# Turning the first two token tiles behind the last expert's second half: float32r transposes in place of float32 identity matmuls

## The chip, the cores and the metric

One core of a Trainium2 chip runs the whole program in one launch. The metric is device time in microseconds of that core; the median of several executions is compared. Engines by their short names: PE is TensorE (PEld its weight loads), DVE VectorE, ACT ScalarE, POOL GpSimd, SP SyncE.

## The reference

Three stages follow one another on 1536 tokens (2 batches of 768) of 512 numbers.

1. A decayed linear attention, 8 heads of 64, gives the rows `x`.
2. A mixture of 8 experts with one expert for each token. `e` is the largest gate logit, or the expert of the token before where the local gate is open:

```python
p = softmax(x[b, s] @ w_gate)
h = np.maximum(x[b, s] @ w1[e], 0.0)        # 512 -> 1024
out[b, s] = p[e] * (h @ w2[e])              # 1024 -> 512
```

3. A mixing stage, for all tokens: `gate = sigmoid(causal 5-tap convolution of x with conv_w)`, `val = x @ w_val`, result `(gate * val) @ w_out`.

The change lies at the seam of stages 2 and 3: the first 256 tokens of stage 3 need their expert's answers, turned so that the 512 features lie on partitions.

## The kernel before

**Experts.** Tokens are sorted by expert into slots (up to 240 slots an expert are computed here, in two tiles of 128). For each expert `e` in 0 to 7, `up(e, j)` makes the hidden rows in four pieces, and `down(e, 0)` and `down(e, 1)` (line 768) make the answers of its first and second tile of slots: 24 matmuls each of 128x128 against 128x512, which add up in one PSUM tile `py`. Numbers are split in a high and a low float32r part, so each product is three float32r matmuls. `down_out` (line 778) scales `py` on ACT into `yo` and writes it to `ys` in HBM by a DMA that ACT issues (line 782).

**The mixing stage** takes the tokens in their own order again, 256 (two tiles) at a time, n = 0 to 5. `fetch(n)` gathers two tiles of answers from `ys` by indirect DMAs that POOL issues (line 907); `turn(n)` transposes them on PE into PSUM (line 917, float32r, through `nc.tensor.transpose`); `parts(n)` splits them (ACT line 928, DVE line 930); `whole(n)` and `taps(n)` feed the convolution, which `conv(n, ...)` adds up on DVE (line 951); `value(n)` is 48 matmuls (line 965), `gate(n)` multiplies, `project(n, t)` is the last product (line 991).

**The first two tiles take a shortcut.** They don't wait until the last expert's answers are in HBM:

- `early_answers` (line 789), during the last expert's `up`, gathers the answers of these 256 tokens that earlier experts gave into `yg` (line 792). Tokens of the last expert get a row of zeros. It also makes two one-hot matrices `oh0` and `oh1` on DVE, which say what token has which slot of the last expert.
- `early_answers_turn` (line 800) turns `yg` into two PSUM tiles `pt0` (line 804): for each of 4 blocks of features and 2 tiles an ordinary float32 matmul of the 128x128 block with the identity `ident`, 8 calls. The first call in a PSUM bank has `start=True`, and none has `stop`.
- `last_parts` (line 807) splits the last expert's first tile of answers into two float32r parts on ACT and DVE, and `last_place(0, ...)` (line 812) adds them to `pt0` through `oh0`: 8 float32r matmuls (line 815). `last_place(1, [yo])` adds the second tile, from `yo`, as 4 float32 matmuls through `oh1`.

`pt0` then stands in for `turn(0)`. The mixing stage begins with `fetch(1)`, then `parts(0)`, `whole(0)`, `taps(0)` and `value(0)`, and `turn(1)` is put into `value(0)` after 40 of its 48 matmuls.

**Order.** In both parts the instructions of PE, ACT, DVE and SP stand in the order in which the code calls them (`manual_schedule`); in the mixing stage POOL does too. Semaphore waits are derived from the tiles that instructions read and write. `fetch(1)` reads all of `ys`, so it waits for the last write of `ys`; this wait stands in semaphore instructions on POOL's queue ahead of the gather. The first gather's own instruction waits for PE's last matmul of line 815.

**The last expert's end**, before (lines 855 to 879), in the order of the calls: `down(7, 0)`, `down_out(7, 0)`, `last_parts`, `early_answers_turn`, `down(7, 1)`, `last_place(0)`, `down_out(7, 1)`, `last_place(1)`.

Of the kernel before, what the change touches and what calls it, by code (L numbers as in the profile page):

```python
# [9 lines left out]
F32R = mybir.dt.float32r  # L10
# [11 lines left out]
P = 128  # L22
# [19 lines left out]
def fused_kernel(ctx, tc, qkv, lam, wgl, w1, w2, wv, cw, wo, out, dbg=None):  # L42
    nc = tc.nc
# [44 lines left out]
    ident = const.tile([P, P], F32, name="ident")  # L88
# [3 lines left out]
    identr = const.tile([P, P], F32R, name="identr")  # L92
# [101 lines left out]
    def from64_b(dst, a, m):  # L194
        nc.vector.scalar_tensor_tensor(dst, m.bitcast(F32), MIN64, a.bitcast(F32), op0=ALU.is_ge, op1=MUL)
# [3 lines left out]
    def split64_a(n):  # L199
        src, c0 = (wv if n < 4 else wo), (n % 4) * 512  # L200
        raw = wraw_p.tile([P, 1024], U32, name="wraw64", tag="wraw")
        nc.sync.dma_start(raw, src[:, c0:c0 + 512].bitcast(U32))
        w64_t[n] = from64_a(raw)

    def split64_b(n):
        dst, c0 = (wv_t if n < 4 else wo_t), (n % 4) * 512
        w = f64_p.tile([P, 512], F32, name="f64w", tag="f64w")
        from64_b(w, *w64_t.pop(n))
        sl = slice(c0, c0 + 512)
        nc.scalar.copy(dst[:, 0, sl], w)  # L210
        nc.gpsimd.tensor_tensor(dst[:, 1, sl], w, dst[:, 0, sl].bitcast(F32), op=SUB)
# [12 lines left out]
    def first_hi(n, cs=slice(0, 1024)):  # L224
        w = (w1_t if n < 4 else w2_t)[0]
        if len(w) == n % 4:
            w.append(split_hi(raw_t[n], None, cs))
        else:
            split_hi(raw_t[n], w[n % 4], cs)

    def first_lo(n, cs=slice(0, 1024)):
        split_lo(raw_t[n], (w1_t if n < 4 else w2_t)[0][n % 4], cs)
# [392 lines left out]
    def all_indices():  # L625
        for g in range(ET, NT):
            indices(g)
        nc.vector.tensor_tensor(idx, idxa, pidx[:, 2 * E:4 * E], op=ADD)
# [85 lines left out]
    def x_fetch(e):  # L714
        xr = xr_p.tile([P, 2, XW], F32, name="xr", tag="xr")
        for t in range(2):
            nc.gpsimd.indirect_dma_start(  # L717
                xr[:, t, :], None, xd, bass.IndirectOffsetOnAxis(ap=idx[:, 2 * e + t:2 * e + t + 1], axis=0))
        xr_t[e] = xr

    def softmax_fetch(e):
        xs = xh_p.tile([P, 2, E], F32, name="xsm", tag="xsm", bufs=1)

        rows = keep.tile([P, 2], I32, name="rows")
        nc.vector.tensor_scalar(rows, idx[:, 2 * e:2 * e + 2], float(XW // E), float(DM // E), op0=MUL, op1=ADD)
        for t in range(2):
            nc.gpsimd.indirect_dma_start(
                xs[:, t, :], None, xd.rearrange("r (a n) -> (r a) n", n=E), bass.IndirectOffsetOnAxis(ap=rows[:, t:t + 1], axis=0))
        return xs
# [13 lines left out]
    def softmax_of(e, xs):  # L743

        pe = xh_p.tile([P, 2], F32, name="pe", tag="pe")
        nc.gpsimd.tensor_copy(pe, xs[:, :, e])
        pe_t[e] = pe

    def w1_chunk(e, k):
        w1_t.setdefault(e, []).append(split(raw_load(w1[e * P:(e + 1) * P, k * FF:(k + 1) * FF])))  # L750

    def w2_chunk(e, j):
        raw = raw_t[4 + j] if e == 0 else raw_load(w2[e * P:(e + 1) * P, j * 1024:(j + 1) * 1024])
        w2_t.setdefault(e, []).append(split(raw))

    def up(e, j, hhs):
        ph = ps_h.tile([P, 2, CAP], F32, name="ph", tag="ph")[:, :, 0:C1]
        xh = xh_t[e]
        for fi, a, b, k, first, last in halves(e == j == 0):
            f = 2 * j + fi  # L760
            nc.tensor.matmul(ph[:, fi, :], w1_t[e][k][:, a, f * P:(f + 1) * P],  # L761
                             xh[:, b, k].rearrange("p t n -> p (t n)")[:, 0:C1], start=first, stop=last)
        hh = hidden[(e * (KF // 2) + j) % len(hidden)]
        nc.scalar.activation(hh[:, 0, :, 0:C1], ph, AF.Relu)  # L764
        nc.vector.scalar_tensor_tensor(hh[:, 1, :, 0:C1], ph, 0.0, hh[:, 0, :, 0:C1].bitcast(F32), op0=ALU.max, op1=SUB)  # L765
        hhs.append(hh)
# [20 lines left out]
    early, pt0 = {}, []  # L787

    def early_answers():
        early["yg"] = yg = whl_p.tile([P, 4, DM], F32, name="yg0", tag="whl")  # L790
        for t in range(2):
            nc.gpsimd.indirect_dma_start(yg[:, t, :], None, ys[0:ZROW + 1, :],
                                         bass.IndirectOffsetOnAxis(ap=yslot0[:, t:t + 1], axis=0))
        early["y"] = whl_p.tile([P, 4, DM], F32R, name="yhl", tag="whl")
        for t in range(2):
            oh = early["y"][:, 2 + t, 0:CAP]
            nc.vector.tensor_scalar(oh, iota256, last[:, t:t + 1], None, op0=ALU.is_equal)
            early[f"oh{t}"] = oh if t == 0 else oh.bitcast(F32)

    def early_answers_turn():  # L800
        pt0.extend(ps_x.tile([P, 2, CAP], F32, name=f"pt{i}", tag="px") for i in range(2))
        for k in range(KD):
            for t in range(2):
                nc.tensor.matmul(pt0[k // 2][:, k % 2, t * P:(t + 1) * P], early["yg"][:, t, k * P:(k + 1) * P], ident,
                                 start=(k % 2 == t == 0), stop=False)

    def last_parts(py):
        y, pe = early["y"], pe_t[E - 1][:, 0:1]
# [3 lines left out]
    def last_place(t, srcs):  # L812
        for k in range(KD):
            for src in srcs:
                nc.tensor.matmul(pt0[k // 2][:, k % 2, :], src[:, k * P:(k + 1) * P], early[f"oh{t}"],  # L815
                                 start=False, stop=(t == k % 2 == 1))

    ordered = {mybir.EngineType.Activation, mybir.EngineType.DVE, mybir.EngineType.PE, mybir.EngineType.SP}
    with tc.manual_schedule(engines=ordered):
        parts_of_answers = answers()  # L820
        for e in range(E):
            hhs = []
            if 0 < e < E - 1:
                x_fetch(e + 1)
            for j in range(KF // 2):
                up(e, j, hhs)
                if e == 0 and j == 0:
                    all_indices()
                    softmax_of(0, softmax_fetch(0))
                    x_fetch(1)  # L830
                    first_hi(5)
                    first_lo(5)
                elif e == 0 and j == 1:
                    nc.sync.dma_start(ys[ZROW:ZROW + 1, :].rearrange("o (a n) -> (o a) n", a=2), zero[0:2, :])
                elif e == 1 and j == 0:

                    nc.scalar.activation(sig, warm_sb[:, 0:1], AF.Sigmoid)
                elif e == E - 1 and j == 1:
                    early_answers()
                if e > 0:  # L840
                    w2_chunk(e, j)
                elif 0 < j < 3:
                    w2_chunk(e, j + 1)
                if 2 <= e < 5 and j == 1:
                    next(parts_of_answers)
                if e == 0 and j == 3:
                    split64_a(0)
                if j == 3 and e > 0:
                    split64_b(e)
                    if e == 3:  # L850
                        nc.sync.dma_start(cw_raw, cw.bitcast(U32))
                        from64_b(cw_sb.rearrange("p k j -> p (k j)"), *from64_a(cw_raw))
            if e + 1 < E:
                w1_chunk(e + 1, 0)
            py = down(e, 0, hhs)
            if e + 1 < E:
                w1_chunk(e + 1, 1)
                x_turn(e + 1)
            down_out(e, 0, py)
            if 1 <= e < 1 + NOV:  # L860
                for t in range(2):
                    r0 = (E + e - 2) * CAP + t * P
                    for c0 in range(0, DM, 256):
                        nc.sync.dma_start(ys[r0:r0 + P, c0:c0 + 256], zero)
            if e == E - 1:
                last_parts(py)
                early_answers_turn()
            py = down(e, 1, hhs)
            if e + 1 < E:
                w1_chunk(e + 1, 2)  # L870
                w1_chunk(e + 1, 3)
                if e == 0:
                    split64_b(0)
                split64_a(e + 1)
            if e == E - 1:
                last_place(0, [early["y"][:, a, :] for a in range(2)])
            yo = down_out(e, 1, py)
            if e == E - 1:
                last_place(1, [yo])
# [317 lines left out]
```

## Time and profile before

| | us |
|---|---|
| median of 3 runs | 346.55 (346.36 to 347.4) |
| profiled execution, its own time | 346.0 |
| its span in the profile | 344.1 |
| PE busy | 334.5 (97%) |
| DVE busy | 272.1 (79%) |
| ACT busy | 197.2 (57%) |
| POOL busy | 65.0 (19%) |

The span is what the profiler saw of engines; 1.9 us of the execution's own time lie around it. The engines work at once, so the busy times don't add up. Ends of matmuls are modelled, and neighbours overlap in the rows, so the distance from start to start is the safer reading of how long a matmul holds PE. A matmul on float32 data shows as two matmuls and two weight loads, one on float32r data as one.

### The profile page before, as it was taken

What the parts mean: (1) busy time and instruction counts of PE and PEld (TensorE: products, weight loads), DVE (VectorE), ACT (ScalarE), POOL (GpSimd) and SP (SyncE); (2) the same over time, 40 slices, a digit from 0 to 9 for tenths busy, and PEclk for the clock granted to TensorE, in tenths of its full rate; (3) what the DMA queues carried; (4) which work ended last, traced back from release to release, by engine and by line L of the source; (5) the groups of instructions that cost most, each with busy time, mean ns of one, the idle gap of its engine ahead of it and who ended that gap; (6) DMA issues with size and microseconds to landing.
All of it is one profiled execution on the core that took longest, in us unless ns stands there. A gap on an engine that the chain in (4) does not pass through costs nothing.

```text
span 344.1 us, 7024 instructions
## 1 busy us (share of the span) xinstructions
PE 334.5 (97%) x2686; PEld 296.4 (86%) x2686; DVE 272.1 (79%) x600; ACT 197.2 (57%) x418; POOL 65.0 (19%) x84
## 2 busy tenths in 40 slices
PE   6999999999999999999999999999999899999995
PEld 3888888879989889899898898998988889899884
DVE  5788999988798688788987877778740799977980
ACT  1577677864557645745756457457441567664731
POOL 3000000020463121321411214201320650000000
PEclk9999999999999999999999999999999999999999
DMA  6997983473778888799698887987521542011012
GB/s 245 403 350 294 302 311 96 126 225 114 225 234 289 275 282 280 235 318 286 196 354 275 270 296 223 356 259 239 198 63 61 139 132 71 35 56 63 30 63 98
DMA packets 24819, 72.00 MB, mean 209 GB/s; under 512 B 3398, under 2 KB 6732, under 8 KB 23628
## 3 DMA queue, kind: packets, MB, share of 16 engines
q1 hardware_dynamic: 20020, 59.87, 51.5%
q0 software_dynamic: 2304, 7.42, 7.4%
q10 hardware_dynamic: 2456, 4.20, 3.2%
q8 instruction: 23, 0.38, 0.5%
q14 instruction: 16, 0.13, 0.1%
HBM read 57.79 MB, written 13.68 MB: 208 GB/s over the span
## 4 chain that ended last, share of the span: by engine, by line
PE 91%; DMA 3%; DVE 2%; ACT 1%; SPq 0%; issue 0%; POOL 0%; ACTq 0%
PE py L773 26%; PE ph L761 25%; PE po L991 10%; PE pv L965 9%; PE ps L273 4%; PE po L297 3%; PE po L290 3%; PE rt L337 2%; PE rt L335 2%; DMA qk<-in_qkv_dram 2%; PE st L317 1%; PE px L737 1%; DMA yg<-ys,yslot 1%; PE pt L917 1%; PE pt L815 1%; PE px L450 1%
## 5 line engine op out<-in xcount | busy, mean ns | idle before, releaser
L168 DVE TENSOR_TENSOR whl<-wraw,whl 128x1024 fp32r<-128x1024 f32 (+1 forms) x68 | 81.8, 1219 | 17.5 <-ACT whl L164 17.5
L773 PE MATMUL py<-whl,hh 128*128 128x512 f32 x384 | 92.7, 396 | 0.0
L761 PEld LDWEIGHTS ph<-xh,whl 128*128 128x128 f32 x768 | 87.8, 190 | 1.1 <-ACT xh L473 0.4
L761 PE MATMUL ph<-xh,whl 128*128 128x240 f32 x768 | 88.4, 276 | 0.2 <-ACT xh L473 0.2
L773 PEld LDWEIGHTS py<-whl,hh 128*128 128x128 f32 x384 | 70.9, 188 | 16.0
L164 ACT CAST whl<-wraw 128x1024 fp32r<-128x1024 f32 (+1 forms) x68 | 66.3, 994 | 4.7 <-ACT yo L780 2.9
L764 ACT ACTIVATE hh<-ph 128x480 fp32r<-128x480 f32 x32 | 18.3, 573 | 41.3 <-PE ph L761 40.6
L951 DVE SCALAR_TENSOR_TENSOR gt<-yt,cw_sb,gt 128x256 f32<-128x256 f32 x96 | 39.0, 476 | 1.1 <-ACT gt L943 1.1
L965 PE MATMUL pv<-yh,wv_t 128*128 128x256 f32 x288 | 35.6, 283 | 0.0
L965 PEld LDWEIGHTS pv<-yh,wv_t 128*128 128x128 f32 x288 | 35.1, 191 | 0.5 <-ACT yh L928 0.2
L991 PE MATMUL po<-wo_t,gh 128*128 128x512 f32 (+1 forms) x156 | 34.6, 378 | 0.0
L991 PEld LDWEIGHTS po<-wo_t,gh 128*128 128x128 f32 x156 | 27.3, 188 | 5.8 <-DVE gh L981 0.8
L765 DVE SCALAR_TENSOR_TENSOR hh<-ph,hh 128x480 fp32r<-128x480 f32 x32 | 21.0, 656 | 12.8 <-ACT hh L764 12.8
L780 ACT ACTIVATE yo<-py,pe 128x512 f32<-128x512 f32 x16 | 11.1, 695 | 18.7 <-PE py L773 18.7
L717 POOL DMA_INDIRECT xr<-xd,idx x14 | 16.6, 1186 | 12.5 <-PE px L737 6.9
L273 PE MATMUL ps<-qk 64*128 64x128 f32 x176 | 15.3, 295 | 0.0
L443 POOL DMA_INDIRECT xr<-xd,idx x2 | 2.7, 1338 | 64.5 <-DMA wraw<-in_w_dram 64.2
L191 POOL TENSOR_TENSOR f64a<-f64a,f64s 128x512 f32<-128x512 f32 (+1 forms) x9 | 12.4, 1380 | 10.8 <-DMA wraw<-in_w_dram 9.1
L907 POOL DMA_INDIRECT yg<-ys,yslot x10 | 11.2, 1121 | 17.1 <-DVE yh L930 11.2
L280 DVE TENSOR_TENSOR sm<-ps,dm 128x512 f32<-128x512 f32 x22 | 14.1, 681 | 0.2 <-PE ps L273 0.2
L928 ACT CAST yh<-pt 128x512 fp32r<-128x512 f32 x12 | 6.6, 588 | 11.7 <-PE pt L917 10.3
L297 PE MATMUL po<-sm,qk 128*64 128x128 f32 x192 | 13.1, 279 | 0.0
(175 smaller groups left out, 426.1 us busy)
## 6 DMA issues: line engine op xcount, KB each, us to landing
wraw<-in_w_dram SPq DMA_DIRECT2D x64, 512.0 KB, 5.8
qk<-in_qkv_dram SPq DMA_DIRECT2D x9, 1024.0 KB, 5.9
ys<-yo ACTq DMA_DIRECT2D x16, 256.0 KB, 6.2
xd<-xtok SPq DMA_DIRECT2D x12, 260.0 KB, 2.5
ys<-warm_sb SPq DMA_DIRECT2D x24, 128.0 KB, 5.1
out_dram<-oo SPq DMA_DIRECT2D x11, 256.0 KB, 2.0
qk<-in_qkv_dram SPq DMA_DIRECT2D x5, 512.0 KB, 6.2
wraw<-in_w_val_dram SPq DMA_DIRECT2D x4, 512.0 KB, 4.7
```

The source lines that it names most:

```text
L164: nc.scalar.copy(hl[:, 0, cs], raw[:, cs])
L168: nc.vector.tensor_tensor(hl[:, 1, cs], raw[:, cs], hl[:, 0, cs].bitcast(F32), op=SUB)
L273: nc.tensor.matmul(ps_t[g][hl][:, hp, :], t[r, half, 256 + c0:256 + c0 + P], t[r, half, c0:c0 + P], start=True, stop=True)
L297: nc.tensor.matmul(po_t[g][hl * D:(hl + 1) * D, hp, :], qk_t[g][:, 3, h * D:(h + 1) * D], sm_t[g][:, hl, hp, :], start=(c == 0), stop=(c = ...
L717: nc.gpsimd.indirect_dma_start(xr[:, t, :], None, xd, bass.IndirectOffsetOnAxis(ap=idx[:, 2 * e + t:2 * e + t + 1], axis=0))
L761: nc.tensor.matmul(ph[:, fi, :], w1_t[e][k][:, a, f * P:(f + 1) * P], xh[:, b, k].rearrange("p t n -> p (t n)")[:, 0:C1], start=first, sto ...
L764: nc.scalar.activation(hh[:, 0, :, 0:C1], ph, AF.Relu)
L765: nc.vector.scalar_tensor_tensor(hh[:, 1, :, 0:C1], ph, 0.0, hh[:, 0, :, 0:C1].bitcast(F32), op0=ALU.max, op1=SUB)
L773: nc.tensor.matmul(py, hhs[f // 2][:, a, f % 2, t * P:(t + 1) * P], w2_t[e][f // 2][:, b, (f % 2) * DM:(f % 2 + 1) * DM], start=(n == 0), ...
L951: nc.vector.scalar_tensor_tensor(gt[:, k, :], yt[:, b, k, c0 + j:c0 + j + 256], cw_sb[:, k, j:j + 1], gt[:, k, :], op0=MUL, op1=ADD)
L965: nc.tensor.matmul(pv[:, mi, :], wv_t[:, a, k * DM + m * P:k * DM + (m + 1) * P], yh[:, b, k, :], start=first, stop=last)
L991: nc.tensor.matmul(po, gh[:, a, k, t * P:(t + 1) * P], wo_t[:, b, k * DM + cs.start:k * DM + cs.stop], start=(i == 0), stop=(i == 11))
```

## The change

`early_answers_turn` is called later, between `down(7, 1)` and `last_place(0)`, and its 8 calls are float32r transposes (`is_transpose=True` against `identr`, views of the same bytes as float32r) with the same `start` and `stop` flags. The `last_place` matmuls add to what the transposes left in PSUM, as they did to what the matmuls left. No other call is moved.

```diff
         for k in range(KD):
             for t in range(2):
-                nc.tensor.matmul(pt0[k // 2][:, k % 2, t * P:(t + 1) * P], early["yg"][:, t, k * P:(k + 1) * P], ident,
-                                 start=(k % 2 == t == 0), stop=False)
+                nc.tensor.matmul(pt0[k // 2][:, k % 2, t * P:(t + 1) * P].bitcast(F32R),
+                                 early["yg"][:, t, k * P:(k + 1) * P].bitcast(F32R), identr,
+                                 start=(k % 2 == t == 0), stop=False, is_transpose=True)
...
             if e == E - 1:
                 last_parts(py)
-                early_answers_turn()
             py = down(e, 1, hhs)
...
             if e == E - 1:
+                early_answers_turn()
                 last_place(0, [early["y"][:, a, :] for a in range(2)])
             yo = down_out(e, 1, py)
```

## Rows read from the trace of the kernel before

**Rows 1.** The page: busy times, and the chain that ended last by engine.
```profile
PE 334.5 (97%) x2686; PEld 296.4 (86%) x2686; DVE 272.1 (79%) x600; ACT 197.2 (57%) x418; POOL 65.0 (19%) x84
...
PE 91%; DMA 3%; DVE 2%; ACT 1%; SPq 0%; issue 0%; POOL 0%; ACTq 0%
```

**Rows 2.** The chain of waits in order of time: start, length, engine, tile, line, count.
```profile
142.92 0.64 PE px L737 x8
143.56 5.67 PE py L773 x24
...
165.66 0.63 PE px L737 x8
...
256.54 1.78 PE pt L804 x16
258.32 5.61 PE py L773 x24
263.93 2.79 PE pt L815 x16
...
268.79 4.37 DMA yg<-ys,yslot
...
273.81 6.77 PE pv L965 x56
```

**Rows 3.** Line 815, from `yo`: count, duration ns min/median/max, first and last start.
```profile
L815 PE MATMUL pt<-yhl,yo x8: 379/379/475, 264.7 to 266.3; 128*128 128x256 f32 x8
```

**Rows 4.** Line 737, the float32r transposes of the experts' rows.
```profile
L737 PE MATMUL px<-identr,xr x56: 221/248/255, 96.8 to 234.2; 128*128 128x128 f32 x56
```

**Rows 5.** Timeline around the seam: start, length, instructions [idle before <-releaser].
```profile
263.77 1.11 PE L815 MATMUL pt<-yhl 128*128 128x256 f32 x8
263.97 0.69 ACT L780 ACTIVATE yo<-py,pe 128x512 f32<-128x512 f32 x1 [5.56 <-PE py L773]
264.69 0.33 ACTq L782 DMA_DIRECT2D ys<-yo  x1
...
264.72 1.99 PE L815 MATMUL pt<-yhl,yo 128*128 128x256 f32 x8
...
266.51 5.02 PE L965 MATMUL pv<-yh,wv_t 128*128 128x256 f32 x40
...
266.78 1.27 DVE L930 TENSOR_TENSOR yh<-pt,yh 128x512 fp32r<-128x512 f32 x2
...
267.53 0.96 POOL L907 DMA_INDIRECT yg<-ys,yslot  x1 [11.15 <-DVE yh L930]
...
271.37 0.46 PE L917 MATMUL pt<-identr,yg 128*128 128x128 f32 x4
...
272.49 0.69 DVE L930 TENSOR_TENSOR yh<-pt,yh 128x512 fp32r<-128x512 f32 x1
...
273.30 0.51 PE L917 MATMUL pt<-identr,yg 128*128 128x128 f32 x4 [1.47 <-DMA yg<-ys,yslot]
...
274.46 0.69 DVE L930 TENSOR_TENSOR yh<-pt,yh 128x512 fp32r<-128x512 f32 x1 [1.28 <-ACT yh L928]
```

**Rows 6.** Line 782 (255 to 268 us), the last expert's writes: issue to landing.
```profile
DMA to landing us min/median/max: 2.0/2.0/2.0
```

**Rows 7.** Line 907 (266 to 272 us): POOL's queue, and landings.
```profile
L907 POOLq EVENT_SEMAPHORE  x3: 17/43/43, 266.7 to 270.9; - x3
...
DMA to landing us min/median/max: 3.3/3.8/4.4
```

**Rows 8.** POOL's timeline: two other gathers released by PE.
```profile
144.33 1.50 POOL L717 DMA_INDIRECT xr<-xd,idx  x1 [1.58 <-PE px L737]
...
166.56 1.54 POOL L717 DMA_INDIRECT xr<-xd,idx  x1 [0.67 <-PE px L737]
```

**Rows 9.** Line 717 (142 to 146 us): the queue instruction ahead of the first of these.
```profile
L717 POOLq EVENT_SEMAPHORE  x1: 17/17/17, 143.6 to 143.6; - x1
```

**Rows 10.** Stretches: length, busy (count) of PE, PEld, DVE, ACT, POOL; PEclk, DMA, GB/s.
```profile
233.60:234.40 0.80, 0.80 (x10) 0.74 (x9) 0.80 (x1) 0.80 (x2) 0.06 (x1) 1.00 0.53 164
```

## The prediction

> **What bounds the kernel now.** I read the busy table first, then the chain of waits, then the timeline of the few microseconds around the edit. PE is busy 97% of the span and is 91% of the chain that ended last [rows 1]; a microsecond of PE work that is taken out anywhere on that chain is a candidate for a microsecond of time. The chain around the edit [rows 2] shows where that is true. From 256.54 to 266.7 it is PE without a gap: the 16 passes of line 804 (1.78 us), the second half of the answers (5.61), the placing of line 815 (2.79). Then it leaves PE: it goes through a gather of the next two tiles from HBM (4.37 us from issue to landing), and comes back to PE at the second half of that tile pair's transposes. The timeline [rows 5] shows the same as a wait: PE does its 40 matmuls of line 965, transposes the first gathered tile at 271.37, and then stands idle 1.47 us until the second tile has landed (273.30). From there on the chain is PE again.
>
> So there are two things to follow through the edit: how much earlier PE reaches that wait, and how much earlier the wait ends. The later of the two sets the end.
>
> The timeline names DVE line 930 as the releaser of the first gather (267.53). I don't believe it: the gather is called before that line and depends on nothing that it writes. What it does depend on is the last write of `ys`, issued at 264.69 [rows 5], landed 2.0 us later [rows 6], at 266.69; and POOL's first semaphore instruction for it runs at 266.7 [rows 7]. The other condition is PE's last placing, which ends at 264.72 + 1.99 = 266.71. Both fall together today, and the gather starts 0.83 after them.
>
> **Part 1, removed: 16 passes ahead of the second half.** 1.78 us by the chain [rows 2], 0.11 a pass. Nothing hides them: the second half follows on PE with no idle time, and what it needs (hidden rows, weights, its PSUM tile) was there for the first half. So the second half ends 1.78 earlier, and with it `yo`, the write of `ys`, and its landing: 266.69 - 1.78 = 264.91. Neither ACT nor DVE has an instruction moved, and `last_parts`, which depends on the first half only, is done long before PE comes to its product.
>
> **Part 2, added: 8 float32r transposes behind the second half.** The trace has the same instruction between the same neighbours, the transposes of the experts' rows: eight take 0.63 to 0.64 on the chain, in 7 groups (56 in all [rows 4]) of which two are shown [rows 2], and the product after them shows 5.67 where the one behind line 804 shows 5.61: 0.06 for a weight load that isn't ahead. I take 0.70. Bounds: 0.63 from below; from above 8 x 0.248 = 1.98, if none overlapped the next [rows 4], or 1.78 if they cost what they cost as float32. The nearest row is the same shape, type and mode, hence 0.70. Their data is there, since line 804 works on it at 256.54 today, and so are the PSUM tiles, so they wait for nothing. They lie on PE's path, behind the second half, and delay `last_place(0)`.
>
> **Part 3, a wait that goes.** The 4 calls of the second placing need `yo`. Today ACT makes it from 263.97 to 264.66, while PE does the first placing; the `yo` matmuls start at 264.72 [rows 5], and the first of the eight takes 475 ns where the median is 379 [rows 3]: about 0.10 lost because its weights couldn't be loaded ahead. After the edit PE has 0.70 more to do in the same place, so `yo` is early by some 0.6, and I take the 0.10 as gained. Bounds: 0 to 0.10.
>
> **The sum on PE.** `pt0` is complete 1.78 - 0.70 + 0.10 = 1.18 earlier, at 265.53; the 40 matmuls end, and PE stands ready for the second gathered tile, 1.18 earlier.
>
> **The sum at the gather.** Its two conditions part: the write of `ys` lands 1.78 earlier (264.91), the placing ends 1.18 earlier (265.53). What counts is how soon the gather starts after each. With a semaphore instruction ahead, the start comes late: the gather at 144.33 follows the end of the transposes that released it (142.92 + 0.64 = 143.56) by 0.77, its queue instruction ran at 143.6 [rows 2, 8, 9]. The gather at 166.56 had no such instruction last; it waited by itself, and started 0.27 after its release (165.66 + 0.63 = 166.29). By the first, the new start is 264.91 + 0.83 = 265.74; by the second, 265.53 + 0.27 = 265.80. The later is 265.80, against 267.53: 1.73 earlier. The second gather is issued behind it and lands 1.73 earlier, as the DMA queues hold the same transfers in the same order.
>
> **The end.** PE is ready 1.18 earlier and the tile lands 1.73 earlier, so the wait of 1.47 shrinks to about 0.9 and still sets the end: everything behind moves by 1.73. DVE agrees: its second split (274.46) waits for the same tile, and its first (272.49 to 273.18), which moves by 1.18, ends at 272.00, before the new 272.73. The profiled execution took 346.0 of its own (span 344.1 and 1.9 around it), and would take 344.3. The median of the runs shown is 0.55 above it; from that, 346.55 - 1.73 = 344.8, which I forecast.
>
> **A rule that speaks against it.** The transposes of line 737 start 0.08 apart, and the stretch around eight of them shows a granted clock of 1.00 [rows 10], the 2.4 GHz level. The Trainium skill, page "TensorE: Matmul & The Clock Gate", section "Part 4: PE-mode transpose", gives about 275 ns for a transpose in one kernel, and says that the fast clock doesn't engage for them. By that figure eight would be an estimated 2.2 us, more than the 1.78 removed. The trace doesn't agree on either count, for a burst between dense matmuls. It is the reason why the fourth rival stands below.
>
> **The rivals.**
> 1. The gather moves with PE alone: its start keeps its 0.82 after the end of the placing (267.53 - 266.71), whatever the write of `ys` does. Then it starts at 266.35, and the end moves 1.18: 345.4. For it: the two conditions coincide today, so the trace can't tell which one counted. Against it: 0.27 in the row without a queue instruction.
> 2. The change doesn't do what it says: moved, but not cheaper (1.78 for the eight, because they are to be added to, or 1.98 unoverlapped). The placing ends 0.10 earlier or later than today, the gather by its 0.27 starts at 266.88 or 267.08, and 0.65 or 0.45 are left: about 346.0, within what can be told. Against it: the rows of line 737.
> 3. The gather's landing has its own luck: 3.3 to 4.4 us in this stretch [rows 7]. If the second tile comes early, PE waits for nothing; the most there is to win is 1.18 + 1.47 = 2.65, or 343.9.
> 4. Slower: PE falls to the 1.2 GHz level with the transposes. Its work from there to the second gathered tile is 0.70, then the placing less its lost 0.10 (2.69), then the 40 matmuls (4.86 from 266.51 to 271.37) and 0.46: 8.7 us, which would take 8.7 more; PE would come to the tile at about 279.4 in place of 273.3, some 6 us late: 352.6. It turns from gain to loss once more than 1.47 + 1.18 = 2.65 us of this work run at the lower level. Against it: the clock is 1.00 around a burst like it [rows 10], and PE has no idle time here.
>
> **How the numbers follow.** Forecast 0.60, rival 1 0.18, rival 2 0.12, rival 3 (a gain over 2.2) 0.05, rival 4 or anything slower 0.05. The range takes in the forecast, rivals 1 and 2 and part of 3: 344.1 to 346.0. What a measurement can tell here is 0.3%, 1.04 us. Forecast and rival 3 are beyond it nearly always; rival 1 with its 1.18 only six times in ten; rival 2 is not. That gives 0.70 faster, 0.25 the same, 0.05 slower.
>
> **What would show it.** In the profile after: the chain without a transpose between the two halves; eight transposes, 0.6 to 0.7 us, behind the second; no gap before the `yo` matmuls; the first gather of line 907 starting about 0.9 after the landing of `ys` and 0.3 after the last placing; PE's wait before the second gathered tile at 0.9 instead of 1.47 (still 1.47 means rival 1). No wait there at all, a granted clock under 1.00, or sixteen passes where eight are forecast would prove me wrong.

## The result, and the profile after

The changed kernel takes 349.03 us (median of 5 runs, 348.71 to 349.99), against 346.55 before: ratio 1.0074, 95% interval 1.0059 to 1.009. I had forecast 344.8, and even 346.0 as the top of the range. The profiled execution took 348.71 with a span of 346.8, 2.71 more than the one before.

In the chain of waits after (columns as in [rows 2]; lines behind 806 are one higher than before: 816 is the placing, 908 the gather, 918 the transposes of gathered tiles, 929 their split on ACT, 966 the value product) the edit itself is as forecast, and then something new stands in the chain:

```profile
251.07 11.20 PE py L773 x48
262.27 0.65 PE pt L804 x8
262.91 2.76 PE pt L816 x16
...
269.23 5.19 another core or an unknown queue
...
274.44 1.08 ACT yh L929 x2
...
275.57 8.42 PE pv L966 x48
283.99 0.64 PE pt L918 x8
284.62 5.52 PE po L992 x24
```

The two halves of the answers now stand together (48 matmuls), eight transposes take 0.65, the placing 2.76 [rows 2: 1.78 and 2.79]. The gather that held the chain in [rows 2] is gone from it. In its place ACT waits 5.19 us for what the view can't name (the kernel runs on one core, so it is not another core). And 48 matmuls of line 966 take 8.42 us where the groups further on in the same trace take 5.75.

The timeline after, around the seam, answers to [rows 5]:

```profile
262.31 0.69 ACT L780 ACTIVATE yo<-py,pe 128x512 f32<-128x512 f32 x1 [3.77 <-PE py L773]
...
263.02 0.33 ACTq L782 DMA_DIRECT2D ys<-yo  x1
...
265.93 0.97 POOL L908 DMA_INDIRECT yg<-ys,yslot  x1 [9.43 <-DVE yt L900]
...
269.71 0.95 POOL L908 DMA_INDIRECT yg<-ys,yslot  x1 [0.30 <-DMA yg<-ys,yslot]
...
270.37 0.46 PE L918 MATMUL pt<-identr,yg 128*128 128x128 f32 x4
270.97 1.21 POOL L908 DMA_INDIRECT yg<-ys,yslot  x1 [0.30 <-issue]
...
271.08 0.51 PE L918 MATMUL pt<-identr,yg 128*128 128x128 f32 x4 [0.25 <-DMA yg<-ys,yslot]
...
271.43 1.19 PE L966 MATMUL pv<-yh,wv_t 128*128 128x256 f32 x8
272.48 0.95 POOL L908 DMA_INDIRECT yg<-ys,yslot  x1 [0.30 <-issue]
274.44 1.07 ACT L929 CAST yh<-pt 128x512 fp32r<-128x512 f32 x2 [5.21 <-remote]
274.68 0.95 POOL L908 DMA_INDIRECT yg<-ys,yslot  x1 [1.25 <-remote]
...
275.57 8.42 PE L966 MATMUL pv<-yh,wv_t 128*128 128x256 f32 x48 [2.95 <-ACT yh L929]
```

Read it from below. PE waits 2.95 us for ACT's split of the gathered tiles (275.57). ACT starts this at 274.44. It waits for one thing in the program, the report (the semaphore increment that rides on the last transpose) that the first tile is turned. That transpose ended at 270.37 + 0.46 = 270.83; before, ACT followed within 0.04 (271.37 + 0.46 = 271.83, split at 271.87). Now it follows 3.61 later. POOL's seventh gather (274.68) waits for the same report, and it starts 0.24 behind ACT, as gathers that wait by themselves do [rows 8]. So it isn't ACT that is late: two engines are let go at the same moment. I call this a held report. (Ends of matmuls are modelled, so the rows can't tell a report that was sent late from one that arrived late.)

The second effect follows from the first. Stretches of the trace (columns as in [rows 10]):

```profile
266.00:272.40 6.40, 6.15 (x54) 6.04 (x53) 4.30 (x10) 3.06 (x7) 4.96 (x5) 1.00 0.55 156
272.40:275.60 3.20, 0.25 (x3) 0.04 (x2) 0.54 (x1) 1.07 (x2) 1.87 (x2) 0.79 0.60 182
275.60:281.10 5.50, 5.50 (x26) 5.50 (x27) 5.50 (x15) 3.94 (x7) 0.98 (x2) 0.50 0.37 99
281.10:285.00 3.90, 3.90 (x35) 3.81 (x35) 3.90 (x9) 1.90 (x4) 0.45 (x1) 1.00 0.00 0
```

The granted clock is 1.00 through the transposes, and falls while PE is idle. When PE starts again it works 5.5 us at 0.50, the 1.2 GHz level, before it has 1.00 back. The Trainium skill, page "TensorE: Matmul & The Clock Gate", section "HAM oscillation — how this bites in real kernels", describes a clock that falls while PE waits for transfers, and a slow start behind the wait. The trace shows the same pattern, with a wait on a report.

The sum, against the forecast: 2.95 of idle time, 8.42 - 5.75 = 2.67 for the slower product, less 0.49 because PE came to the second tile at 271.08 and not at the forecast 271.57: 5.13 at the end of this product. Some 2.4 of the 2.67 are the lower clock: in e4 and r4 below, the same 48 matmuls at a clock of 1.00 take 6.01 and 6.00 behind shorter waits. Before, the same product ended at 273.81 + 6.77 = 280.58 [rows 2]; after at 283.99, 3.41 later; and -1.73 + 5.13 = 3.40. The next product gives 0.65 back, since DVE had time to catch up (5.52 in place of 6.17). What is left, about 2.7, is the 2.71 of the execution.

### The profile page after: what moved, and what is told of

Its sections match the earlier page's. It is cut to its first block, busy times and chain, and to the rows that moved or that the text cites. A ratio compares the mean times of both kernels' runs of the same rounds, so it can differ in the third digit from the quotient of the medians.

```text
span 346.8 us, 7008 instructions
## 1 busy us (share of the span) xinstructions
PE 335.1 (97%) x2678; PEld 297.8 (86%) x2678; DVE 271.2 (78%) x600; ACT 197.7 (57%) x418; POOL 66.4 (19%) x84
## 4 chain that ended last, share of the span: by engine, by line
PE 90%; DVE 4%; ACT 2%; another core or an unknown queue 1%; DMA 1%; issue 0%; ACTq 0%
PE py L773 26%; PE ph L761 25%; PE po L992 10%; PE pv L966 9%; PE ps L273 3%; PE po L297 3%; PE po L290 3%; PE rt L337 2%; PE rt L335 2%; PE st L317 1%; PE px L737 1%; DMA lam_sb<-in_lam_dram 1%; PE pt L816 1%; PE pt L918 1%; DVE dm L107 1%
## 5 line engine op out<-in xcount | busy, mean ns | idle before, releaser
L966 PE MATMUL pv<-yh,wv_t 128*128 128x256 f32 x288 | 38.3, 295 | 3.0 <-ACT yh L929 3.0
L966 PEld LDWEIGHTS pv<-yh,wv_t 128*128 128x128 f32 x288 | 37.6, 204 | 3.7 <-ACT yh L929 3.4
L992 PE MATMUL po<-wo_t,gh 128*128 128x512 f32 (+1 forms) x156 | 33.9, 375 | 0.0
L717 POOL DMA_INDIRECT xr<-xd,idx x14 | 18.6, 1325 | 11.8 <-PE px L737 6.4
L443 POOL DMA_INDIRECT xr<-xd,idx x2 | 2.7, 1338 | 64.7 <-DMA wraw<-in_w_dram 64.4
L931 DVE TENSOR_TENSOR yh<-pt,yh 128x512 fp32r<-128x512 f32 x12 | 7.7, 683 | 9.3 <-ACT yh L929 5.6
L908 POOL DMA_INDIRECT yg<-ys,yslot x10 | 10.2, 1017 | 20.5 <-DVE yt L900 9.4
```

What stands on the lines that cost most here:

```text
L717: nc.gpsimd.indirect_dma_start(xr[:, t, :], None, xd, bass.IndirectOffsetOnAxis(ap=idx[:, 2 * e + t:2 * e + t + 1], axis=0))
L966: nc.tensor.matmul(pv[:, mi, :], wv_t[:, a, k * DM + m * P:k * DM + (m + 1) * P], yh[:, b, k, :], start=first, stop=last)
L992: nc.tensor.matmul(po, gh[:, a, k, t * P:(t + 1) * P], wo_t[:, b, k * DM + cs.start:k * DM + cs.stop], start=(i == 0), stop=(i == 11))
```

## The experiments

Theories at the start: **A**, the hold comes from PE reaching the gathered tiles just as they land; **B**, from float32r transposes that are then added to; **C**, from the late place of the turn in any form; **D**, from where instructions lie. The first four ran on one chip (before: 346.73 there).

**e1: moved only.** The late call, with the old float32 matmuls in it; against the kernel before, only the call moves.

```diff
             if e == E - 1:
                 last_parts(py)
-                early_answers_turn()
             py = down(e, 1, hhs)
...
             if e == E - 1:
+                early_answers_turn()
                 last_place(0, [early["y"][:, a, :] for a in range(2)])
```

> Edit: the turn is called late, as in the change, but stays 8 float32 identity matmuls (16 passes). After the change TensorE finishes the transposes of the first gathered tile at 270.83, but ScalarE, which waits for them, starts at 274.44, and TensorE's clock falls behind that. Theory A (the hold comes from TensorE reaching the gathered tiles just as they land): here TensorE is 1.08 later against the gather, the gather 0.65 earlier than before at most, so no hold, about 346.0. Theory B (float32r transposes that are then added to cause it): no hold, about 346.0. Theory C (the late place causes it, whatever the form): a hold, 349 or more. Theory D (it hangs on where instructions lie in the program): can't say; 346.0 or 349.

349.94, ratio 1.009 (1.0061 to 1.012). The first gathered tile was turned at 271.80 and ACT started at 274.74: held 2.94. B falls, and A as I had worked it out.

**e2: cheaper only.** The transposes, in the old place.

```diff
             if e == E - 1:
                 last_parts(py)
+                early_answers_turn()
             py = down(e, 1, hhs)
...
-                early_answers_turn()
                 last_place(0, ...)
```

> Edit: the 8 float32r transposes stay in the old place, ahead of the second half. All behind them moves by the same 1.78 - 0.70 = 1.08. Theory A: TensorE and the gather keep their distance of before, no hold, 345.5. Theory B: a hold, about 349. Theory C: no hold, 345.5. Theory D: as many instructions as in the change, so a hold if their count decides, 349.

345.57, ratio 0.9962 (0.9946 to 0.9978): 1.16 less than before, where 1.08 was worked out. A small hold is there (tile turned at 270.76, ACT at 271.40, 0.64) and costs nothing, since PE waits 1.57 for the second tile anyway.

**e3: the change, with the gathers later.** GpSimd adds 16 columns of the first split ahead of them, and so waits for it.

```diff
-        for n in range(len(pt0) // 2, 2):
-            fetch(n)
...
         parts(0)
+        if pt0:
+            hold = g_p.tile([P, 16], F32, name="hold", tag="hold", bufs=1)
+            hi = yh_t[0][:, 0, 2, 0:16].bitcast(F32)
+            nc.gpsimd.tensor_tensor(hold, hi, hi, op=ADD)
+        fetch(1)
         whole(0)
```

> Edit: the change, and GpSimd adds 16 columns of the first split in a tile that nobody reads ahead of the first gather, so that this starts about 0.9 later against TensorE, as before the change or a little later (TensorE would then wait about 1.5 to 1.9 for the second tile in place of 0.25). Theory A: no hold, 345.4 to 345.9. Theories B and C: a hold as in the change, about 349 to 350. Theory D: can't say.

345.67, ratio 0.9967 (0.9949 to 0.9986): no costly hold (0.23). C falls: late transposes are there, and no hold worth the name.

**e4: the change, with PE later:** 5 matmuls of 128x512 that nobody reads, ahead of the transposes.

```diff
+        def pad():
+            pd = ps_o.tile([P, DM], F32, name="pad", tag="po2")
+            for i in range(5):
+                nc.tensor.matmul(pd, identr, wo_t[:, 0, 0:DM], start=True, stop=True)
+
-        value(0, lambda: turn(1))
+        value(0, lambda: (pad() if pt0 else None, turn(1)))
```

> Edit: the change, and 5 matmuls of 128x512 that nobody reads (1.17 us) on TensorE ahead of the transposes of the gathered tiles, so that TensorE comes there after both tiles have landed. Theory A in the form that being early does the harm: no hold, about 345.3. Theories B and C: a hold, 349 to 350. Theory D: can't say.

347.88, ratio 1.0033 (1.0015 to 1.0051): both tiles had landed when PE came, and still ACT waited from 271.94 (the first tile's four transposes end at 271.48 + 0.46) to 274.45. A falls. But ACT was let go at 274.45 here and at 274.44 in the changed kernel, though PE was done 1.1 later. The end of the hold seems to hang on something that didn't move between the two: the gathers, which start at 265.88 here and at 265.93 there.

```profile
265.88 0.96 POOL L908 DMA_INDIRECT yg<-ys,yslot  x1 [9.43 <-DVE yt L900]
...
271.48 0.80 PE L918 MATMUL pt<-identr,yg 128*128 128x128 f32 x8
...
274.45 1.07 ACT L929 CAST yh<-pt 128x512 fp32r<-128x512 f32 x2 [5.28 <-PE pv L966]
```

After the two that the seam needs, POOL issues four more without a pause, for later tiles. That is **theory E**: a run of gathers that goes on past PE's report holds the report. The next four ran on another chip, where the kernel before takes 349.42.

**e5: the change, two gathers, and the other pairs held back** by small GpSimd additions that wait for later work.

```diff
+        def hold(src):
+            h = g_p.tile([P, 16], F32, name="hold", tag="hold", bufs=1)
+            nc.gpsimd.tensor_tensor(h, src, src, op=ADD)
...
-        fetch(2)
         conv(0, (1, 2))
         parts(1)
+        if pt0:
+            hold(yh_t[1][:, 0, 0, 128:144].bitcast(F32))
+        fetch(2)
...
+                if pt0 and n == 1:
+                    hold(gt_t[0][:, 0, 0:16])
                 fetch(n + 2)
```

> Edit: the change, and the second and third pair of gathers each wait for a small GpSimd addition (16 columns, read by nobody) that depends on later work, so that only two gathers are issued before TensorE's report on the gathered tiles. Theory E (TensorE's report is held while or after GpSimd issues a run of four and more gathers): no hold, ScalarE starts within 0.1 us of the transposes, and the forecast of the change comes out: 1.7 less than before, 344.6 to 345.2. Theory A (TensorE's early arrival at the gathered tiles does it) or chance by place: the hold stays, 348.5 to 350.

344.47, ratio 0.9882 (0.9821 to 0.9943). Its timeline: transposes, split and product follow each other without a gap, and the third gather starts later.

```profile
266.05 0.96 POOL L908 DMA_INDIRECT yg<-ys,yslot  x1 [9.43 <-DVE yt L900]
...
267.31 0.95 POOL L908 DMA_INDIRECT yg<-ys,yslot  x1 [0.30 <-issue]
...
270.49 0.97 PE L918 MATMUL pt<-identr,yg 128*128 128x128 f32 x8
270.98 1.09 ACT L929 CAST yh<-pt 128x512 fp32r<-128x512 f32 x2 [1.64 <-PE pt L918]
...
271.29 6.93 PE L966 MATMUL pv<-yh,wv_t 128*128 128x256 f32 x56
...
272.52 0.97 POOL L908 DMA_INDIRECT yg<-ys,yslot  x1
```

**e6: only the second pair held back** (the edit against e5). Four gathers follow in a run, but behind the report.

```diff
-                if pt0 and n == 1:
-                    hold(gt_t[0][:, 0, 0:16])
                 fetch(n + 2)
```

> Edit: as e5, but only the second pair of gathers is held back, so that four follow in a run after it. Theory E: no hold at the first report; one may come later, where the run of four has been issued and TensorE reports to VectorE or ScalarE: 344.6 to 347. Theory A: hold as in the change, 348.5 to 350.

344.86, ratio 0.9871 (0.9811 to 0.993); ACT is 0.03 behind the transposes.

**e7: e5, and four gathers that nobody reads** right behind the first two.

```diff
+        if pt0:
+            spare = g_p.tile([P, 4, DM], F32, name="spare", tag="spare", bufs=1)
+            for i in range(4):
+                nc.gpsimd.indirect_dma_start(spare[:, i, :], None, ys, bass.IndirectOffsetOnAxis(ap=yslot[:, 4 + i:5 + i], axis=0))
```

> Edit: e5, and four gathers that nobody reads are issued right behind the first two. Theory E: the run of six is back, and the hold with it: 347.5 to 350, with ScalarE 1 to 3.6 us late at the seam. If it was the place of the second pair of gathers or something else that e5 moved, no hold: 344.6 to 345.4.

349.28, 4.8 more than e5 on the same chip. The run is back, and the hold with it:

```profile
270.55 0.95 POOL L1017 DMA_INDIRECT spare<-ys,yslot  x1 [0.30 <-issue]
...
271.21 0.46 PE L918 MATMUL pt<-identr,yg 128*128 128x128 f32 x4
271.80 1.21 POOL L1017 DMA_INDIRECT spare<-ys,yslot  x1 [0.30 <-issue]
...
273.31 0.95 POOL L1017 DMA_INDIRECT spare<-ys,yslot  x1 [0.30 <-issue]
275.42 1.07 ACT L929 CAST yh<-pt 128x512 fp32r<-128x512 f32 x2 [5.35 <-remote]
...
276.60 3.81 PE L966 MATMUL pv<-yh,wv_t 128*128 128x256 f32 x20 [3.19 <-issue]
```

Turned at 271.67, let go at 275.42: 3.75. Nothing reads these four gathers, so no data dependency is in play.

**e8: e5, and four plain transfers from SyncE** of the same size, in place of e7's gathers.

```diff
+        if pt0:
+            spare = g_p.tile([P, 4, DM], F32, name="spare", tag="spare", bufs=1)
+            for i in range(4):
+                nc.sync.dma_start(spare[:, i, :], ys[ZROW + 1 + P:ZROW + 1 + CAP, :])
```

> Edit: e5, and four plain transfers of the same size (256 KB each, read by nobody) from SyncE's queue at the same time. Theory E with GpSimd's issuing as the cause: no hold, 344.6 to 345.6. If it is the traffic that holds the report: a hold, 347.5 to 350.

347.08, ratio 0.9932 (0.9904 to 0.9961): 2.6 more than e5, in the middle between the theories' numbers. The profiled execution took 352.39, over 5 above the median, so its times say little (in it, ACT is 0.04 behind the transposes, and PE waits 1.52 and 1.42 for the gathered tiles). Inconclusive by itself; s3 asks the question again.

Four more on a third chip (before: 349.5). **r1: the changed kernel again.**

> The changed kernel once more, on the chip of the next three. Theory E: the hold is there, 348.5 to 350; whether the kernel before has it too on this chip (349.4 on one chip, 346.7 on another so far) shows in its own time.

348.39, ratio 0.9974 (0.9953 to 0.9996). The hold is there (turned at 271.56, ACT at 275.32). On this chip the change is not slower than the kernel before, because that one takes 3 us more here.

**r2: e5 again.**

> The change with the second and third pair of gathers held back, once more. Theory E: no hold, 344.2 to 345.0, whatever the kernel before does on this chip.

344.96, ratio 0.9873 (0.9851 to 0.9895), reports on time.

**r3: the kernel before with e5's edits, without the change.**

> Edit: the kernel before (no change), with the second and third pair of gathers held back as in e5. Theory E: no hold on any chip, so 346.0 to 346.6, less where the run of gathers had cost something; the change on top of this is then worth 1.2 to 1.8 (forecast 1.73). If holding the gathers back were itself the gain, this one would come near 344.5.

347.2, ratio 0.9932 (0.9917 to 0.9948). Beside r2 this is what the change is worth where no report is held: 347.2 - 344.96 = 2.24 by the medians, 346.82 - 345.12 = 1.70 by the two profiled executions (forecast 1.73). I had expected 346.0 to 346.6, so this one missed; and holding the gathers back without the change is worth 2.3 on this chip.

**r4: the change, the run broken** by additions that wait for nothing.

```diff
+        if pt0:
+            hold(iota256[:, 0:16])
         fetch(2)
...
+                if pt0 and n == 1:
+                    hold(iota256[:, 0:16])
                 fetch(n + 2)
```

> Edit: the change, and a small GpSimd addition that waits for nothing (16 columns of a constant) ahead of the second and of the third pair of gathers, so that the run is broken but as many gathers are issued, 0.2 to 0.6 us later each pair. If an unbroken run is needed: no hold, 344.5 to 345.5. If the number of gathers in a few microseconds decides: a hold, 348 to 350.

345.79, ratio 0.9893 (0.9873 to 0.9913). A shorter hold: the first tile is turned at 270.88, and PE waits 1.23 behind it, with no loss of clock.

```profile
270.14 0.95 POOL L908 DMA_INDIRECT yg<-ys,yslot  x1 [0.30 <-issue]
...
270.42 1.05 PE L918 MATMUL pt<-identr,yg 128*128 128x128 f32 x8
...
271.10 0.36 POOL L1010 TENSOR_TENSOR hold<-iota 128x16 f32<-128x16 f32 x1
...
271.61 0.97 POOL L908 DMA_INDIRECT yg<-ys,yslot  x1 [0.16 <-issue]
272.58 1.07 ACT L929 CAST yh<-pt 128x512 fp32r<-128x512 f32 x2 [3.31 <-PE pv L966]
...
273.71 6.00 PE L966 MATMUL pv<-yh,wv_t 128*128 128x256 f32 x48 [1.23 <-issue]
```

The hold is 1.70. An unbroken run isn't needed; breaking it halves the hold.

The last ones ran where the kernel before takes 346.4. **s1 and s5: the kernel before**, for its profile.

> The kernel before, for its profile on this chip. Theory E: where its time is about 349, its profile shows a report of TensorE 1 to 4 us late behind a run of gathers and the clock at half speed behind that; where it is about 346.6, none.

> The kernel before, on another chip if this one is another. Theory E: if its time is about 349 here, its profile shows a report of TensorE 1 to 4 us late behind a run of gathers, and the clock at half speed behind that; if it is about 346.5, none is late by more than 0.7.

346.31 and 346.29. In s1 ACT starts 0.03 behind both tiles. In s5 it starts 0.62 behind the first (turned at 271.74, ACT at 272.36) and 0.03 behind the second; PE waits 1.57 for the second tile anyway, so this costs nothing:

```profile
271.28 0.46 PE L917 MATMUL pt<-identr,yg 128*128 128x128 f32 x4
271.43 0.95 POOL L907 DMA_INDIRECT yg<-ys,yslot  x1 [0.30 <-issue]
272.36 0.58 ACT L928 CAST yh<-pt 128x512 fp32r<-128x512 f32 x1 [2.17 <-PE pt L917]
```

So a small hold is there without the change too, and the same program has it in one execution and not in another, with the report 0.31 behind the start of the fourth gather in both. Neither run fell on a chip where this kernel takes 349.5, so what costs 3 us there was not seen.

**s2: three gathers, the others held back; s4: four.** The edit of s2 against the changed kernel (the third pair is held as in e5; s4 has that hold alone):

```diff
-        def fetch(n):
-            yg_t[n] = []
-            for t in range(2):
+        def fetch(n, ts=(0, 1)):
+            yg_t.setdefault(n, [])
+            for t in ts:
...
+        fetch(2, (0,))
...
-        fetch(2)
         conv(0, (1, 2))
         parts(1)
+        if pt0:
+            hold(yh_t[1][:, 0, 0, 128:144].bitcast(F32))
+        fetch(2, (1,))
```

> Edit: the change, three gathers in a run and the others held back as in e5. If a run of four is needed: no hold, 344.4 to 345.2. If three suffice: a report late by 0.5 us or more.

> Edit: the change, four gathers in a run, the third pair held back. If the run has to go on past the report for a long hold: a report late by less than 1.7 us, 344.5 to 346. If four suffice for the full hold: 347.5 to 350.

344.96, ratio 0.9957 (0.9938 to 0.9976), and 344.89, ratio 0.9955 (0.9938 to 0.9973); reports on time in both (0.04). In s4 the run ends just before the report, at the same distance as in the changed kernel, where a fifth gather follows:

```profile
269.67 0.94 POOL L908 DMA_INDIRECT yg<-ys,yslot  x1 [0.30 <-issue]
...
270.33 1.11 PE L918 MATMUL pt<-identr,yg 128*128 128x128 f32 x8
270.83 1.24 ACT L929 CAST yh<-pt 128x512 fp32r<-128x512 f32 x2 [1.64 <-PE pt L918]
...
271.27 6.94 PE L966 MATMUL pv<-yh,wv_t 128*128 128x256 f32 x56
...
277.76 0.97 POOL L908 DMA_INDIRECT yg<-ys,yslot  x1 [0.15 <-issue]
```

**s3: e7 with plain transfers**, issued by GpSimd.

```diff
-            nc.gpsimd.indirect_dma_start(spare[:, i, :], ...)
+            nc.gpsimd.dma_start(spare[:, i, :], ys[ZROW + 1 + P:ZROW + 1 + CAP, :])
```

> Edit: e7 with plain transfers: the change, two gathers, and four plain transfers of 256 KB that nobody reads, issued from GpSimd's queue behind them. If anything that GpSimd issues in a run holds the report: a hold, 347.5 to 350. If only gathers do: reports on time, 344.5 to 347.5 (the transfers compete with the gathers, as in e8, where that cost some 2).

345.41, ratio 0.9965 (0.9948 to 0.9983), reports on time: ACT starts 0.04 behind the transposes (271.13 and 271.17).

```profile
268.45 2.25 POOL L1017 DMA_DIRECT2D spare<-ys  x4
...
270.67 0.97 PE L918 MATMUL pt<-identr,yg 128*128 128x128 f32 x8
271.17 1.09 ACT L929 CAST yh<-pt 128x512 fp32r<-128x512 f32 x2 [1.64 <-PE pt L918]
```

It isn't the traffic of 1 MB: the DMA engines are busy 0.90 of the microsecond around the report (271 to 272), and 0.80 and 0.62 of the two in the changed kernel (270 to 272). But GpSimd issues a plain transfer in 0.6 us and had issued all four by 270.70, before the report, as it had the four gathers of s4. So it isn't shown that only gathers do it; plain transfers still being issued at the report were not tried.

All traces side by side: how late ACT starts behind the transposes of the first gathered tile, and what the fifth gather does.

| run | ACT late by, us | fifth gather of the run |
|---|---|---|
| before, s1 | 0.04, 0.03 | 0.94 behind the report |
| e2, s5, e3 | 0.64, 0.62, 0.23 | 0.94, 0.95 and 1.40 behind it |
| change, r1, e7, e1 | 3.61, 3.76, 3.75, 2.94 | 0.1 behind it |
| e4 | 2.51 | being issued |
| r4 (spaced) | 1.70 | 0.7 behind it |
| e5, e6, r2, r3, s2, s4, s3 | 0.03 to 0.04 | none, or much later |

## Why the prediction was wrong

**What held, step by step.** The chain starts 0.12 later in this execution (251.07 for 250.95), which is taken off here. Part 1: `yo` starts 1.66 + 0.12 = 1.78 earlier, as forecast. Part 2: eight transposes take 0.65, at 0.08 apiece, and the clock is 1.00 over them; the forecast was 0.70 with the joint. So rival 2 fell. The 275 ns of the Trainium skill ("TensorE: Matmul & The Clock Gate", "Part 4: PE-mode transpose") is near what one row lasts here, 0.22 to 0.25, but not what each adds in a burst. Part 3: the `yo` matmuls take 1.89 in place of 1.99, so the 0.10 was gained. The sum on PE: line 966 starts at 265.47 for 266.51, 1.04 + 0.12 = 1.16 earlier (1.18). The sum at the gather: 265.93 for 267.53, 1.60 + 0.12 = 1.72 earlier (1.73), so rival 1 fell too. The second tile came still earlier than that: PE waits 0.25 for it, not 0.9. Its gather took some 3.7 from issue to landing (267.20 to 271.08, less the 0.14 that PE's start follows by in [rows 2]) in place of 4.37; that 0.6 (the 0.49 above and the 0.12 taken off here) is the spread of rival 3, and luck.

**What failed is the step called "The end"**: "the wait of 1.47 shrinks to about 0.9 and still sets the end: everything behind moves by 1.73". It takes for granted that a finished transpose is known at once to the engine that waits for it. In the trace before this was so, 0.04, and I didn't ask under what conditions. The edit moved PE and the gathers against each other, the first gather by 0.56 (1.16 and 1.72) and the fifth by 0.80: it had been issued 0.94 behind the report, and is now 0.14 behind it. The report was held 3.61, PE idled 2.95, and its clock fell, which was one of the signs that I had set for being wrong.

**Shown** is that the later gathers bring the long hold: with them held back it goes (e5, e6, r2, s2, s4), with idle ones in their place it comes back (e7). The plain transfers of s3 don't bring it, but they were issued before the report, as the four gathers of s4 were, which don't bring it either. That the form and the place of the turn have no part in it but for the moment is shown by e1, e2 and e3. With the gathers out of the way the change is worth 1.70 to 2.24 (r2 and r3), and s2 and s4 are 1.44 and 1.51 under the kernel before, so the gain that the sum gives is there.

**Rival 4 named the right symptom for the wrong reason.** The clock did fall, but behind 2.95 of idle time, not with the transposes. I had set 0.05 on anything slower. I weighed PE's own clock in that rival and nothing that lies between two engines.

**Open.** What in the chip holds the report. The order of report and gathers alone doesn't decide it: before, the second tile's report at 273.81 falls between the fifth and the sixth gather and is on time (273.84); and with the first report 0.31 behind the start of the fourth gather, ACT is on time in two executions (before and s1) and late in two (s5 and e2). Before, s1 and s5 are one program, so theory D, the place of instructions, doesn't decide it either. Where the hold was short, ACT started as the gather then being issued ended: 271.40 in e2, 272.36 for 272.38 in s5, 272.58 in r4; no run tests whether that is the rule. Also open is why the kernel before takes 349.5 on two chips; r3, which is 2.3 faster there, says that the gathers behind the first two have a part in it, but no profile of the kernel before was taken there. That kernel's executions there point the same way: the 26 of 36 that take 349.0 or more show a mean granted clock of 0.988 to 0.995, the ten shorter ones 0.998 to 1.00. So the change is slower by 0.7% where the kernel before takes 346.6, and not slower where it takes 349.5.

**A version that beats both.** The change with the later gathers held back: 344.47, 344.86 and 344.96 where the kernel before takes 349.4 to 349.5 (e5, e6, r2), and 344.89 where it takes 346.4 (s4).

## What to carry to other kernels

When an edit moves one engine against another by half a microsecond, list what else is in flight at the meeting point, and not only the two that meet: a run of prefetching gathers that nobody needs yet can cost more than the edit gains. Issue the gathers that the next step needs, and let the others wait for a later event; here one small GpSimd instruction does that. Before believing that a time is the kernel's own, run it on a second chip.

## What the runs showed of the hardware

- By the rows, a report that rides on a finished matmul can reach other engines up to 3.76 us late while GpSimd goes on issuing gathers (r1); small additions of 16 columns in the right places on GpSimd, which hold the later gathers back, took 3.4 us off on one chip (r1 348.39, r2 344.96). The Trainium skill, page "PSUM — Partial Sum Buffer", section "Engine vs sequencer instructions", says that increments attached to an engine's instruction fire on its completion. Here the waiting engines were let go behind the completion, but up to 3.76 us behind it; no run shows when the increment itself fired.
- Four plain transfers from the same queue, issued before the report and in flight at it, do not do this (1 MB, ACT 0.04 behind, s3).
- A TensorE wait of 2.95 us between dense products cost another 2.4 or so through the clock; waits of 1.2 to 1.6 (r4, r3, e2) and one of 2.27 (e4) cost none. The cost isn't the same each time: 3.24 (r1) cost 7.51 - 6.00 = 1.5, with the clock still at 1.00 when TensorE started again at 276.45.
- The kernel before takes 346.3 to 346.7 on some chips and 349.4 to 349.5 on two; the change with two gathers takes 344.5 to 345.0 on each of those two.
